# Identity products in an accumulator's unused columns, a new order on VectorE and GpSimd in the first unit, and an early load of a weight block: an attention and mixture-of-experts kernel on one core

## The chip, the cores and the metric

The kernel runs on one core of a Trainium2 chip. The metric is the device time of one execution in microseconds. Three executions took 1271.86, 1272.38 and 1274.48 us; the median is 1272.38 us.

## What is computed

The reference packs keys and values of each head into 32 tokens by an attention with learned queries `p`, lets the real queries attend to these 32, and sends the result through a mixture of four experts whose gates `domain_probs` are given.

```python
def sm_attn(qq, kk, vv):
    s = scale * np.matmul(qq, kk.transpose(0, 1, 3, 2))
    a = np.exp(s - np.max(s, axis=-1, keepdims=True))
    a = a / (np.sum(a, axis=-1, keepdims=True) + 1e-09)
    return np.matmul(a, vv)
p_packed = sm_attn(p, k, v)
x = sm_attn(q, p_packed, p_packed)      # then heads beside each other: (N, D)
...
gate = domain_probs / (domain_probs.sum(-1, keepdims=True) + 1e-09)
for e in range(E):
    h = np.maximum(x @ w1[e], 0.0)
    out += gate[:, e:e + 1] * (h @ w2[e])
```

There are 8 batches, 8 heads, 576 positions and head width 64, so 4608 tokens of width 512; 4 experts of inner width 1024. All is fp32.

## The kernel before

**Products.** Every large matrix product is made of three fp32r products: an operand is split into a high part (a cast) and a low part (operand minus high part). `hi_of` (L149) and `lo_of` (L154) record the two steps, `x` becomes `xh` and `xl`, and so on.

**Units.** The eight blocks of 512 inner columns (`ch`, four experts by two) and the eight batches make units `(pair of batches, ch, batch)`, written out in `units` (L403). The first four are (block 0, batch 0), (block 1, batch 0), (block 1, batch 1), (block 0, batch 1). A unit has a first product and a second.

The first is `x @ w1` for 288 tokens (`c`, a half of a batch) and 256 inner columns (`kh`), a group of 12 matmuls, by `mm1_group` (L422). `w1` is not taken raw: since x is made of the 32 packed tokens, `g_form` (L370) multiplies the packed tokens with `w1` to a gate matrix `ghl`, and the groups multiply `ghl` with the softmax weights `xh` and `xl`. VectorE then multiplies by the gate (`pbt`) and takes the maximum with zero in one instruction. The four results are the blocks a11, a12, a21 and a22 of the hidden matrix.

The second product is by Strassen's scheme in Winograd's form: seven products (`product`, L535, 12 matmuls each) instead of eight, of sums s1 to s4 of the a blocks (formed at the end of `mm1_group` in the branch a21) with sums t1 to t4 of the four blocks of `w2` (`t_form`, L504). `ORDER` (L35) is the order of the seven: a11, s3, s1, s2, a22, s4, a12. `s_operand` (L472) splits a left operand: the cast on ScalarE, the subtraction on GpSimd (`st`). a12's operand, `stl`, is split on VectorE (`split`, L414). `tt` are the right operands, `rw` the raw blocks of `w2`. Each product is added into one of seven sums `acc` by VectorE, or copied by ScalarE the first time.

**Start.** Before unit 0, `pack_unit` (L187) packs the tokens of batch 0 (transposes of the weights `a`, copies `at`, products with the values `vt`), and `tok_halves` (L303) forms batch 0's softmax weights in two halves of 288 tokens: `turned`, `shifted` and `normed` are a transpose, row maximum and subtraction, and the normalisation. Batch 1's packing (`packs[2:]`) and its tokens (`tok_unit`, L267) come between: as long as unit 0 runs, `back` (L724) hands out two of their steps behind each product.

**Who comes first.** The tile framework schedules each engine's instructions by its own estimate, within the dependences; several wrappers add an order where the schedule is to be fixed. `InOrder` (L61) keeps VectorE (`vq`) or GpSimd (`gq`) in the order of recording while its `on` is set. `vec` notes the last instruction that forms a unit's blocks as "sum"; `avec` is for attention and, while `avec.on` is set, stays behind the last "sum" recorded so far; `bact` does so on ScalarE behind the last "high" part of `s_operand`, and `bpool` on GpSimd behind the last "low" part. TensorE's groups are kept in order by `together` (L121) and `on_pe` (L108). There are four accumulators of two PSUM banks each (`dbl`); a group uses columns 0 to 287 of both banks of 512. `FORM` (L739) tells behind which products of a unit a step of `t_form` for a later block is recorded, `GROUPS_LATE` (L738) behind which products of unit 1 the groups of unit 2 stand (the first behind product 3). SP issues the loads and stores in the order of recording where they wait for the same buffers.

Of the kernel before, what the change touches and what calls it, by code (L numbers as in the profile page):

```python
# [8 lines left out]
F32 = mybir.dt.float32  # L9
# [7 lines left out]
P = 128  # L17
# [4 lines left out]
NG = NPAIR // 2  # L22
SB = B // 2
HS = S // 2
# [9 lines left out]

ORDER = ["a11", "s3", "s1", "s2", "a22", "s4", "a12"]  # L35
NPROD = len(ORDER)


@with_exitstack
def attention_moe(ctx: ExitStack, tc: tile.TileContext, q, k, v, p, dp, w1, w2, out):  # L40
# [7 lines left out]
    xpool = pool("xpool", 2)  # L48
# [27 lines left out]
    vq, gq = InOrder(nc.vector), InOrder(nc.gpsimd)  # L76
# [226 lines left out]
    def tok_halves(b, new):  # L303
        xs[b] = tuple(xpool.tile([P, NG, 2, HP], F32R, name=f"{n}{b // 2 % 2}") for n in ("xh", "xl"))
        qts = []
        for g in range(NG):
            qts.append(new[g](b, [P, 2, S], "qt"))
            nc.sync.dma_start(out=qts[g], in_=q[b][:, 2 * g:2 * g + 2, :])
        yield
        pss = [  # L310
            scores([b], g, lambda b, pr, hh: ppbd[b % 4][hh * D:(hh + 1) * D, pr, :], {b: qts[g]})[b]
            for g in range(NG)
        ]
        yield
        n = HS // 32
        a2s = [new[g](b, [P, 2 * n, NPK], "a1") for g in range(NG)]
        ats = [new[g](b, [P, S], "at") for g in range(NG)]
        def block(g, c):
            return a2s[g][:, c * n:(c + 1) * n]

        def turned(g, c):
            vq.transpose(out=block(g, c).rearrange("p a n -> p (a n)"), in_=pss[g][:, c, 0:HS])

        def shifted(g, c):
            a2 = block(g, c)
            m2 = small.tile([P, n, 1], F32, name="m2")
            vq.tensor_reduce(out=m2, in_=a2, axis=AX.X, op=ALU.max)
            vq.tensor_tensor(out=a2, in0=a2, in1=m2.broadcast_to([P, n, NPK]), op=ALU.subtract)
            nc.scalar.activation(out=a2, in_=a2, func=AF.Exp, scale=SCALE)

        def normed(g, c):
            a2, ts = block(g, c), slice(c * HS, (c + 1) * HS)
            s2 = small.tile([P, n, 1], F32, name="s2")
            vq.tensor_reduce(out=s2, in_=a2, axis=AX.X, op=ALU.add)
            vq.tensor_scalar_add(s2, s2, 1e-9)
            vq.reciprocal(out=s2, in_=s2)
            vq.tensor_tensor(out=a2, in0=a2, in1=s2.broadcast_to([P, n, NPK]), op=ALU.mult)
            vq.transpose(out=ats[g][:, ts], in_=a2.rearrange("p a n -> p (a n)"))
            xh, xl = (t[:, g, c, 0:HS] for t in xs[b])
            hi_of(xh, ats[g][:, ts], nc.scalar)  # L340
            lo_of(xl, ats[g][:, ts], xh, gq)

        for g in range(NG):
            turned(g, 0)
            shifted(g, 0)
        yield
        normed(0, 0)
        for g in range(NG):
            turned(g, 1)
        normed(1, 0)  # L350
        yield
        for g in range(NG):
            shifted(g, 1)
        yield
        for g in range(NG):
            normed(g, 1)
        yield

    def w1_load(ch):
# [52 lines left out]
    blocks = {}  # L412
# [6 lines left out]
        lo_of(st[:, 1], psv, st[:, 0], vec)  # L419
        blocks[u, "op", ORDER.index(name) if name in ORDER else name] = st  # L420

    def mm1_group(u, kh, c):  # L422
        sb, ch, b = units[u]
        xh, xl = xs[b]
        ts = slice(c * HS, (c + 1) * HS)
        ps = dbl()
        for fi in range(2):
            f = 2 * kh + fi
            fs = slice(f * P, (f + 1) * P)
            n = 0  # L430
            for g in range(NG):
                ghl = gs[b, ch][g]
                for hl, rx in ((0, xl), (0, xh), (1, xh)):
                    mm(
                        out=ps[:, fi, 0:HS], lhsT=ghl[:, hl, fs], rhs=rx[:, g, c, 0:HS],
                        start=n == 0, stop=n == 3 * NG - 1,
                    )
                    n += 1
        psv = ps[:, :, 0:HS]

        def held(name):
            tag, bufs = ("ablk", 3) if name[0] == "a" else ("sblk", 4)
            blocks[u, name] = hpool.tile([P, 2, HS], F32, name=tag, bufs=bufs)
            return blocks[u, name]

        def add(dst, x, y, op):
            vec.tensor_tensor(out=dst, in0=x, in1=y, op=op)

        name = f"a{c + 1}{kh + 1}"
        vec.scalar_tensor_tensor(  # L450
            out=held(name) if c == kh else psv, in0=psv, scalar=0.0,
            in1=pbt[b][:, ts].rearrange("p (o t) -> p o t", o=1).broadcast_to([P, 2, HS]),
            op0=ALU.max, op1=ALU.mult,
        )
        if u == len(units) - 1:
            if c != kh:
                split(u, name, psv)
        elif name == "a21":
            add(held("s3"), blocks[u, "a11"], psv, ALU.subtract)
            add(psv, psv, blocks[u, "a22"], ALU.add)  # L460
            add(held("s2"), psv, blocks[u, "a11"], ALU.subtract)
            nc.scalar.copy(out=held("s1"), in_=psv)  # L462
            if (u, "a12") in blocks:
                add(held("s4"), blocks[u, "a12"], blocks[u, "s2"], ALU.subtract)
        elif name == "a12":
            if (u, "s2") in blocks:
                add(held("s4"), psv, blocks[u, "s2"], ALU.subtract)
            else:
                blocks[u, "a12"] = psv
            split(u, name, psv)  # L470

    def s_operand(u, i):  # L472

# [30 lines left out]
    def t_form(ch, first=False):  # L504
# [7 lines left out]
        steps = (  # L512
            ("a11", "t1", "t3"), ("s3", "s1", "t2"), ("s2", "t4"), ("a22",), ("s4",), ("a12",),
        )
        how = {"t1": ("b12", "b11", "b11"), "t2": ("b22", "t1", "t1"), "t3": ("b22", "b12", "b12"), "t4": ("t2", "b21", "t2")}
        for names in steps:
            for name in names:
# [135 lines left out]
    def drain(gen):  # L653
        for _ in gen:
            pass
# [6 lines left out]
    with ExitStack() as first:  # L662
# [42 lines left out]
            next(gen)  # L705
        next(halves)
        drain(fold)
        next(halves)
        next(forms)
        mm1_group(0, 0, 0)  # L710
        s_operand(0, 0)
        next(halves)
        mm1_group(0, 1, 0)
        for gen in packs[2:]:
            next(gen)
        mm1_group(0, 1, 1)
        mm1_group(0, 0, 1)
        s_operand(0, 1)
        vq.on = gq.on = False
        drain(forms)  # L720

    apool = ctx.enter_context(tc.tile_pool(name="apool", bufs=2, reuse_waits="tile"))

# [12 lines left out]
    GROUPS = {1: ((0, 0),), 3: ((1, 1),), 4: ((0, 1),), 6: ((1, 0),)}  # L736
    GROUPS_FIRST = {2: ((0, 0),), 3: ((1, 1),), 4: ((0, 1),), 6: ((1, 0),)}
    GROUPS_LATE = {3: ((0, 0),), 4: ((1, 1),), 5: ((0, 1),), 6: ((1, 0),)}  # L738
    FORM = {0: (0, 2, 3, 4, 5, 6), 2: (6,), 3: (0, 1, 2, 3, 4)}  # L739
    for kh in range(2):  # L740
        w2_load(1, kh, raw_tile)
    tsteps = nothing
    kind = None
    sums, late, back = nothing, False, second_batch()
    for u, (sb, ch, b) in enumerate(units):
        pos = u % (2 * NCH)
        odd = pos % 2 == 1
        opening = u < 4
        nxt = units[u + 1] if u + 1 < len(units) else None

        if u == 1:
# [26 lines left out]
        for i in range(NPROD):  # L778
# [23 lines left out]
                next(back, None)  # L802
            elif i == 5 and kind != "scores" or i == 2 and u > 2 or i == 0 and odd and u > 3:
                kind = next(back, None)
            if i in form_at:
                next(tsteps, None)
            if u == 1 and i < 2:
                w2_load(2, i, raw_tile)
# [54 lines left out]
```

## Time and profile before

| | |
|---|---|
| three executions | 1271.86, 1272.38, 1274.48 us |
| the profiled execution: time, span | 1272.35 us, 1270.6 us |
| mean granted TensorE clock | 0.997 |
| TensorE busy | 1247.0 us (98%) |
| VectorE, ScalarE, GpSimd busy | 926.1 us (73%), 496.1 (39%), 735.8 (58%) |
| moved by DMA | 213.98 MB, 168 GB/s on average |

The page and the views that answer to questions name engines PE (TensorE matmul), PEld (its weight load), DVE (VectorE), ACT (ScalarE), POOL (GpSimd) and SP (which issues DMAs). A row of the timeline is start, duration, engine, line, operation, `out<-in`, shape and count, and in brackets the idle time ahead of it with the instruction that ended it. A line can be that of a wrapper (L68, L116), so rows are told apart by their tiles.

### The profile page before, as it was taken

To read this page: it belongs to the slowest core of one execution; us is meant where nothing else is said; L and a number is where in the kernel's file an instruction comes from. 1 tells how busy PE (TensorE), PEld (TensorE's weight loads), DVE (VectorE), ACT (ScalarE), POOL (GpSimd) and SP (SyncE) were. 2 spreads that over 40 slices of the span, in tenths; PEclk is the share of its full clock that TensorE was granted. 3 is DMA by queue.
4 is the path that set the end of the run, shared out by engine and by line. 5 is a ranking of instruction groups with operands and counts; after the bars stand their busy time and mean duration, and the time that the engine had idled before them with its cause. 6 is when DMAs were issued, how large, how long until landed. Compare 5 with 4: busy or idle time off the path is not lost.

```text
span 1270.6 us, 26902 instructions
## 1 busy us (share of the span) xinstructions
PE 1247.0 (98%) x10732; PEld 1166.7 (92%) x10732; DVE 926.1 (73%) x1389; ACT 496.1 (39%) x847; POOL 735.8 (58%) x529
## 2 busy tenths in 40 slices
PE   6899999999999999999999999999999999999998
PEld 3789899999999999999999999999999999999998
DVE  6675676788876667888777676788877567766766
ACT  2554445344435233343335433243343533323331
POOL 3876978798675344455466344364557545445456
PEclk9899999999999999999999999999999999999999
DMA  9665575536466444555345555433445543444322
GB/s 339 242 250 200 218 236 177 193 123 213 161 211 209 163 160 127 181 175 165 125 150 175 175 196 165 159 115 116 159 159 182 159 139 116 123 151 159 126 67 76
DMA packets 86508, 213.98 MB, mean 168 GB/s; under 512 B 8816, under 2 KB 27632, under 8 KB 86384
## 3 DMA queue, kind: packets, MB, share of 16 engines
q1 hardware_dynamic: 85712, 212.11, 50.3%
q8 instruction: 86, 1.41, 0.5%
q14 instruction: 38, 0.31, 0.1%
q10 hardware_dynamic: 672, 0.15, 0.1%
HBM read 173.35 MB, written 38.87 MB: 167 GB/s over the span
## 4 chain that ended last, share of the span: by engine, by line
PE 91%; POOL 2%; DMA 2%; DVE 2%; issue 1%; ACT 0%; SPq 0%; DVEq 0%; POOLq 0%; ACTq 0%
PE dbl L116 85%; PE dbl L124 6%; POOL st L68 1%; DMA rw<-in_w 1%; PE dbl L119 1%; DMA pbt<-pnd 1%; DMA vt<-in_v 1%; DVE a L68 1%; POOL tt L68 1%; POOL acc L68 0%; DVE dbl L68 0%; DVE sblk L68 0%; DVE s L68 0%; POOL rw L68 0%; ACT st L151 0%
## 5 line engine op out<-in xcount | busy, mean ns | idle before, releaser
L116 PE MATMUL dbl<-st,tt 128*128 128x288 f32 x4608 | 665.7, 295 | 3.5 <-DVE acc L68 1.8
L116 PEld LDWEIGHTS dbl<-st,tt 128*128 128x128 f32 x4608 | 623.1, 188 | 38.6 <-POOL st L68 19.2
L68 POOL TENSOR_TENSOR st<-sblk,st 128x576 fp32r<-128x576 f32 x252 | 364.7, 1458 | 435.9 <-ACT st L151 434.6
L116 PE MATMUL dbl<-xh,ghl 128*128 128x288 f32 x2048 | 414.4, 295 | 0.0
L68 DVE TENSOR_TENSOR acc<-dbl,acc 128x576 f32<-128x576 f32 x390 | 292.3, 750 | 93.0 <-PE dbl L116 90.6
L116 PEld LDWEIGHTS dbl<-xh,ghl 128*128 128x128 f32 x2048 | 328.9, 189 | 0.2 <-DVE ghl L68 0.2
L116 PE MATMUL dbl<-xl,ghl 128*128 128x288 f32 x1024 | 303.3, 296 | 6.0 <-POOL xl L68 5.7
L151 ACT CAST st<-sblk 128x576 fp32r<-128x576 f32 x252 | 164.1, 675 | 362.6 <-DVE sblk L68 290.9
L68 POOL TENSOR_TENSOR st<-ablk,st 128x576 fp32r<-128x576 f32 x128 | 187.2, 1463 | 47.8 <-ACT st L151 47.7
L116 PEld LDWEIGHTS dbl<-xl,ghl 128*128 128x128 f32 x1024 | 193.1, 189 | 8.7 <-POOL xl L68 6.4
L68 DVE SCALAR_TENSOR_TENSOR dbl<-dbl,pbt 128x576 f32<-128x576 f32 x128 | 97.8, 764 | 75.7 <-PE dbl L116 74.5
L68 DVE SCALAR_TENSOR_TENSOR ablk<-dbl,pbt 128x576 f32<-128x576 f32 x128 | 96.4, 753 | 65.5 <-PE dbl L116 63.0
L151 ACT CAST st<-ablk 128x576 fp32r<-128x576 f32 x128 | 86.1, 674 | 123.7 <-PE dbl L116 92.4
L116 PE MATMUL dbl<-stl,tt 128*128 128x288 f32 x780 | 114.6, 296 | 0.0
L116 PEld LDWEIGHTS dbl<-stl,tt 128*128 128x128 f32 x780 | 105.9, 188 | 0.2
L68 DVE TENSOR_TENSOR ghl<-dbl,ghl 128x512 fp32r<-128x512 f32 x128 | 84.9, 685 | 25.9 <-ACT ghl L151 25.9
L151 ACT CAST ghl<-dbl 128x512 fp32r<-128x512 f32 x128 | 72.2, 590 | 52.9 <-DVE ghl L68 52.2
L68 POOL TENSOR_TENSOR tt<-rw,tt 128x512 fp32r<-128x512 f32 x57 | 74.2, 1321 | 18.7 <-ACT tt L85 18.7
L68 DVE TENSOR_TENSOR stl<-dbl,stl 128x576 fp32r<-128x576 f32 x64 | 48.4, 756 | 39.5 <-ACT stl L151 39.5
L124 PE MATMUL dbl<-wraw,ppbd 64*32 64x512 f32 x1024 | 67.7, 595 | 0.9 <-DMA wraw<-in_w 0.9
L462 ACT COPY sblk<-dbl 128x576 f32<-128x576 f32 x63 | 40.4, 642 | 64.1 <-DVE sblk L68 64.1
L552 ACT COPY acc<-dbl 128x576 f32<-128x576 f32 x56 | 35.9, 641 | 50.9 <-PE dbl L116 50.8
(64 smaller groups left out, 703.1 us busy)
## 6 DMA issues: line engine op xcount, KB each, us to landing
tt<-td SPq DMA_DIRECT2D x175, 512.0 KB, 4.3
wraw<-in_w SPq DMA_DIRECT2D x132, 256.0 KB, 4.3
td<-tt SPq DMA_DIRECT2D x56, 512.0 KB, 5.0
pbt<-pnd SPq DMA_DIRECT2D x32, 288.0 KB, 3.9
out<-acc SPq DMA_DIRECT2D x31, 288.0 KB, 2.6
rw<-in_w SPq DMA_DIRECT2D x16, 512.0 KB, 5.8
kt<-in_k SPq DMA_DIRECT2D x14, 576.0 KB, 5.2
kt<-in_q SPq DMA_DIRECT2D x14, 576.0 KB, 5.8
```

Of the source, the lines that this page charges most:

```text
L68: res = getattr(self.eng, op)(*args, **kw)
L116: on_pe(nc.tensor.matmul(**kw))
L119: on_pe(nc.tensor.transpose(**kw))
L124: ins = nc.tensor.matmul(**kw).ins
L151: return eng.copy(out=dst, in_=src)
L462: nc.scalar.copy(out=held("s1"), in_=psv)
L552: nc.scalar.copy(out=accs[b, i], in_=psv)
```

## The change

- **Identity products.** `mm1_group` takes a number `idle`. For the group of a12 in unit 0 it is `IDLE = 23`: so many fp32 products of the identity with itself, 128 columns wide, go to columns 288 to 415 of the second bank of a12's accumulator, which nothing reads. They are recorded with `together` behind that group, so the two groups of the second token half stay behind them, and a12's multiply on VectorE, which works on the same tile, waits for the last of them.
- **Order of VectorE and GpSimd in the first unit.** a11's operand and a12's split are recorded later, `normed` of the second half is cut in two steps, `t_form`'s second step is cut in two for block 0, and operands 1 to 3 of unit 0 are recorded before the rest of block 0's `t_form`. `avec.on` is set before unit 0 and stays set, `bact.on` is set for the rest of block 0's `t_form` only, and `gq.on` stays set through unit 0. Block 1's `t_form` steps stand behind products 3, 3, 4, 5, 6 and 6 of unit 0 instead of 0, 2, 3, 4, 5 and 6.
- **Block 1's W2.** Its two raw halves go to the two buffers named `xh1`, which hold batch 1's keys, instead of the buffers `rw0` and `rw1` that hold block 0's.

```diff
+IDLE = 23
@@ tok_halves
-        yield
-        for g in range(NG):
-            normed(g, 1)
+        normed(0, 1)
+        yield
+        normed(1, 1)
@@ mm1_group(u, kh, c, idle=0)
+        if idle:
+            together([
+                dict(out=ps[:, 1, HS:HS + P], lhsT=ident, rhs=ident, start=True, stop=True) for _ in range(idle)
+            ])
...
                 add(held("s4"), psv, blocks[u, "s2"], ALU.subtract)
+                split(u, name, psv)
             else:
                 blocks[u, "a12"] = psv
-            split(u, name, psv)
@@ t_form
+        if first:
+            steps = steps[:1] + (("s3", "s1"), ("t2",)) + steps[2:]
@@ before unit 0
         drain(fold)
+        next(forms)
         next(halves)
         next(forms)
         mm1_group(0, 0, 0)
+        next(halves)
         s_operand(0, 0)
-        next(halves)
-        mm1_group(0, 1, 0)
+        mm1_group(0, 1, 0, IDLE)
+        next(forms)
         for gen in packs[2:]:
             next(gen)
+        split(0, "a12", blocks[0, "a12"])
         mm1_group(0, 1, 1)
         mm1_group(0, 0, 1)
-        s_operand(0, 1)
-        vq.on = gq.on = False
+        for i in range(1, 4):
+            s_operand(0, i)
+        avec.on = bact.on = True
+        vq.on = False
         drain(forms)
+        bact.on = False
...
-    FORM = {0: (0, 2, 3, 4, 5, 6), 2: (6,), 3: (0, 1, 2, 3, 4)}
+    FORM = {0: (3, 3, 4, 5, 6, 6), 2: (6,), 3: (0, 1, 2, 3, 4)}
     for kh in range(2):
-        w2_load(1, kh, raw_tile)
+        w2_load(1, kh, lambda shape, name: xpool.tile(shape, F32, name="xh1"))
@@ each unit
+        gq.on = u == 0
...
-            if i in form_at:
+            for _ in range(form_at.count(i)):
                 next(tsteps, None)
```

The order of the built instructions shows where they come to stand. The first place is VectorE while unit 0 ends and unit 1's a21 is formed; `a_781` and `a_793` are batch 1's two token tiles, `m` their row maxima, `s` their row sums. Before:

```order
L68 STREAM_TRANSPOSE a_781<-dbl 128x288 x2
L68 TENSOR_REDUCE m_837<-a_781 128x18
L68 STREAM_TRANSPOSE a_793<-dbl 128x288 x2
L68 TENSOR_TENSOR a_781<-a_781,m_837 128x576
L68 TENSOR_REDUCE m_841<-a_793 128x18
L68 TENSOR_TENSOR a_793<-a_793,m_841 128x576
L68 SCALAR_TENSOR_TENSOR dbl<-dbl,pbt 128x2x288
L68 TENSOR_REDUCE s_867<-a_781 128x18
L68 TENSOR_TENSOR sblk<-ablk,dbl 128x576
L68 TENSOR_TENSOR dbl<-dbl,ablk 128x2x288
```

After, at the same place (the tiles are `a_792` and `a_804`):

```order
L69 STREAM_TRANSPOSE a_792<-dbl 128x288 x2
L69 STREAM_TRANSPOSE a_804<-dbl 128x288 x2
L69 SCALAR_TENSOR_TENSOR dbl<-dbl,pbt 128x2x288
L69 TENSOR_TENSOR sblk<-ablk,dbl 128x576
L69 TENSOR_TENSOR dbl<-dbl,ablk 128x2x288
L69 TENSOR_TENSOR sblk<-dbl,ablk 128x576
L69 TENSOR_REDUCE m_856<-a_792 128x18
L69 TENSOR_REDUCE m_860<-a_804 128x18
L69 TENSOR_TENSOR a_792<-a_792,m_856 128x576
L69 SCALAR_TENSOR_TENSOR dbl<-dbl,pbt 128x2x288
L69 TENSOR_TENSOR a_804<-a_804,m_860 128x576
```

The maxima and subtractions moved from ahead of a21's multiply (the first `SCALAR_TENSOR_TENSOR`) to behind it and the three sums that follow from it.

The second place is VectorE a little later, where the finished tokens are transposed into `at` and unit 1's products are added into `acc`. Before, from the addition of product 0 on:

```order
L68 TENSOR_TENSOR acc_574<-dbl,acc_574 128x576
L68 STREAM_TRANSPOSE at<-a_781 128x576
L68 TENSOR_TENSOR ghl<-dbl,ghl 128x512
L68 TENSOR_TENSOR stl<-dbl,stl 128x2x288
L68 TENSOR_TENSOR ghl<-dbl,ghl 128x512
L68 TENSOR_TENSOR acc_638<-dbl,acc_638 128x576
L68 TENSOR_TENSOR acc_703<-dbl,acc_703 128x576
L68 TENSOR_TENSOR acc_752<-dbl,acc_752 128x576
L68 STREAM_TRANSPOSE at<-a_793 128x576
```

After, from the same `ghl` on; between the addition of product 0 (`acc_603`) and these rows stand the row sums `s` of both tiles and `stl`:

```order
L69 TENSOR_TENSOR ghl<-dbl,ghl 128x512
L69 RECIPROCAL s_892<-s_892 128x18
L69 TENSOR_TENSOR ghl<-dbl,ghl 128x512
L69 TENSOR_TENSOR acc_659<-dbl,acc_659 128x576
L69 TENSOR_TENSOR a_792<-a_792,s_887 128x576
L69 TENSOR_TENSOR a_804<-a_804,s_892 128x576
L69 TENSOR_TENSOR acc_721<-dbl,acc_721 128x576
L69 STREAM_TRANSPOSE at<-a_792 128x576
L69 TENSOR_TENSOR acc_763<-dbl,acc_763 128x576
L69 STREAM_TRANSPOSE at<-a_804 128x576
```

The first `at` moved from behind the addition of product 0 to behind that of product 2, the second stays behind that of product 3.

The third place is ScalarE in batch 1's packing, the two pairs of copies `at` (whole tile and rest) that TensorE's second pass reads. Before:

```order
L85 COPY at<-dbl 128x512
L85 COPY at<-dbl 64x128
L552 COPY acc_638<-dbl 128x576
L151 CAST st<-sblk 128x2x288
L85 COPY at<-dbl 128x512
```

After:

```order
L86 COPY at<-dbl 128x512
L86 COPY at<-dbl 64x128
L86 CAST tt<-rw_183 128x512 x2
L86 CAST tt<-xh_586 128x512
L559 COPY acc_659<-dbl 128x576
L152 CAST st<-sblk 128x2x288
L86 COPY at<-dbl 128x512
```

Three casts of W2 blocks moved in between the pairs; before, two of them stood ahead of unit 0's first product and one behind the second pair. On GpSimd the subtractions that give the second half's two `xl` moved ahead of a11's `st`, each directly behind a W2 step, and the operands s3, s1 and s2 of unit 0 moved ahead of the last cast and the last three subtractions of block 0's W2.

More of the change, by code (lines that the diff above doesn't have):

```diff
@@ L420, in split, with mm1_group @@
         blocks[u, "op", ORDER.index(name) if name in ORDER else name] = st
-    def mm1_group(u, kh, c):
+    def mm1_group(u, kh, c, idle=0):
         sb, ch, b = units[u]
```

## The prediction

> **What bounds the kernel now.** I read the page first: its span and its busy shares.
>
> ```profile
> span 1270.6 us, 26902 instructions
> PE 1247.0 (98%) x10732; PEld 1166.7 (92%) x10732; DVE 926.1 (73%) x1389; ACT 496.1 (39%) x847; POOL 735.8 (58%) x529
> ```
>
> The profiled execution took 1272.35 us, 1.75 more than its span; the median of the runs shown is 1272.38, so sums made against the profile need no correction. TensorE is busy 98% of the span and sets the time: what it waits, or runs at a slower clock, is lost. So I next asked for the windows view, cut where the start-up ends, and then for the timeline of TensorE there.
>
> ```profile
> 28.50:40.63 12.13, 6.34 (x26) 5.66 (x25) 9.57 (x22) 4.86 (x10) 10.83 (x11) 0.72 0.96 359
> 58.30:85.30 27.00, 25.21 (x204) 22.89 (x193) 22.44 (x35) 12.54 (x21) 20.45 (x15) 1.00 0.85 309
> ...
> 28.09 0.43 PE L116 MATMUL dbl<-xh,ghl 128*128 128x288 f32 x2
> 34.19 0.61 PE L116 MATMUL dbl<-xl,ghl 128*128 128x288 f32 x1 [5.67 <-POOL xl L68]
> 40.63 1.74 PE L116 MATMUL dbl<-st,tt 128*128 128x288 f32 x12
> 49.38 0.65 PE L116 MATMUL dbl<-xl,at 128*32 128x64 f32 x32 [0.96 <-ACT at L85]
> 72.62 4.98 PE L116 MATMUL dbl<-st,tt 128*128 128x288 f32 x36 [1.79 <-DVE acc L68]
> 77.44 0.29 PE L116 MATMUL dbl<-xl,ghl 128*128 128x288 f32 x1
> 81.78 0.29 PE L116 MATMUL dbl<-xl,ghl 128*128 128x288 f32 x1
> ```
>
> The columns of the windows are the length, the busy time of PE, weight load, VectorE, ScalarE and GpSimd, then the granted clock, the DMA share and GB/s. A large loss lies in 28.5 to 40.6: it waits 5.67 us for the second half of batch 0's tokens (`xl`), and then works at a low clock. Later waits are 0.96 at 49.38 and 1.79 at 72.62. At 77.44 and 81.78 it takes up the two halves of batch 1's `xl` without a wait. The 36 products from 72.62 to 77.44 give 0.134 us for one 288-column product at full clock.
>
> **The idle block.** No plain fp32 product of 128 columns stands in the trace. An fp32 product is two records there, so 23 are 46 records. The grouped rows give the length of one record at 512 and at 288 columns.
>
> ```profile
> L124 PE MATMUL dbl<-wraw,ppbd 64*32 64x512 f32 x128 | 13.1, 595 | 0.9 <-DMA wraw<-in_w 0.9
> L124 PE MATMUL dbl<-kt,ppbd 64*32 64x288 f32 x32 | 2.1, 405 | 0.0
> ...
> 44.70 1.31 PE L119 MATMUL dbl<-ident,a 128*128 128x128 f32 x10 [0.48 <-ACT sblk L462]
> ```
>
> 190 ns for 224 columns more is 0.85 ns a column, 0.109 us for 128, 5.0 us for 46. Ten transposes of that width in 1.31 us give 6.0 as the other end. I take 5.2: the block lasts from 28.5 to 33.7, inside the old wait. It adds one wait: a12's multiply on VectorE now waits for its last product. Behind that multiply stand the row maxima of batch 1's first scores, whose exponentials on ScalarE free the accumulator that a21 needs.
>
> **The second half's tokens.** These VectorE and GpSimd rows set the old wait.
>
> ```profile
> 26.87 0.46 DVE L68 TENSOR_TENSOR a<-a,m 128x288 f32<-128x288 f32 x1
> 28.17 0.76 DVE L68 SCALAR_TENSOR_TENSOR ablk<-dbl,pbt 128x576 f32<-128x576 f32 x1 [0.84 <-DMA pbt<-pnd]
> 28.85 0.44 DVE L68 TENSOR_REDUCE s<-a 128x9 f32<-128x288 f32 x1
> 30.02 1.34 DVE L68 TENSOR_TENSOR a<-a,s 128x288 f32<-128x288 f32 x1
> 31.80 0.41 DVE L68 TENSOR_REDUCE s<-a 128x9 f32<-128x288 f32 x1
> 33.52 0.48 DVE L68 STREAM_TRANSPOSE at<-a 128x288 f32<-128x288 f32 x1
> ...
> 36.04 0.74 DVE L68 TENSOR_REDUCE nb<-dbl 128x1 f32<-128x576 f32 x1
> ...
> 37.01 0.74 ACT L85 ACTIVATE a<-dbl,nb 128x576 f32<-128x576 f32 x1 [1.68 <-DVE nb L68]
> ```
>
> Normalising one head group took 2.95 us with a slow `a<-a,s` (28.85 to 31.80) and 2.2 without (31.80 to 34.00). Now it starts at 27.35, with a11's multiply (0.68 to the next start) between the two groups: the second transpose ends between 27.35 + 2 x 2.2 + 0.68 = 32.4 and 33.9. The block's 33.7 and this chain end within 0.3 us of each other, so a12's multiply starts at about 33.9. From there 0.68 to the maxima, 0.97 from them to the exponential, and 0.78 for it: a21's products start at 36.35, and 12 at full clock end at 38.0. Product 0 started at 40.63, so **2.6 us** are won here (2.1 to 2.9 for a block of 6.0 to 5.0 us). GpSimd, which now takes `xl` first, and block a22 are ready before that.
>
> **The casts on ScalarE.** In the second pass of batch 1's packing TensorE waits for the `at` copies. Three casts of W2 blocks now stand between the first pair and the second.
>
> ```profile
> 38.59 1.13 ACT L85 CAST tt<-rw 128x512 fp32r<-128x512 f32 x2
> 46.72 0.75 ACT L85 COPY at<-dbl 128x512 f32<-128x512 f32 x2
> 47.63 0.64 ACT L552 COPY acc<-dbl 128x576 f32<-128x576 f32 x1 [0.16 <-PE dbl L116]
> ```
>
> The first pair ends at 47.47 - 2.6 = 44.87. The casts add 1.7 (1.13 for two), and copy, cast and copy the old 1.75 (47.63 to 49.38): TensorE goes on at 48.3, not 49.38. Of the gain **1.0 us** is left; if the casts cost nothing it would be 2.6.
>
> **VectorE in unit 1.** From 49.38 to 62.66 the old TensorE rows have no wait, so that stretch moves by 1.0. Here the new order on VectorE decides.
>
> ```profile
> 62.23 0.43 PE L116 MATMUL dbl<-xh,ghl 128*128 128x288 f32 x2
> ...
> 58.39 0.85 DVE L68 STREAM_TRANSPOSE a<-dbl 128x288 f32<-128x288 f32 x2 [0.31 <-PE dbl L124]
> 60.70 0.72 DVE L68 TENSOR_TENSOR a<-a,m 128x576 f32<-128x576 f32 x1
> 70.52 1.29 DVE L68 TENSOR_TENSOR a<-a,s 128x576 f32<-128x576 f32 x1
> 72.40 0.76 DVE L68 STREAM_TRANSPOSE at<-a 128x576 f32<-128x576 f32 x1
> 73.09 0.65 DVE L68 TENSOR_TENSOR ghl<-dbl,ghl 128x512 fp32r<-128x512 f32 x1
> 74.93 0.73 DVE L68 TENSOR_TENSOR acc<-dbl,acc 128x576 f32<-128x576 f32 x1
> ...
> 73.19 0.67 ACT L85 CAST xh<-at 128x576 fp32r<-128x576 f32 x1 [1.44 <-DVE at L68]
> 75.83 1.43 POOL L68 TENSOR_TENSOR xl<-at,xh 128x576 fp32r<-128x576 f32 x1
> ```
>
> Before, VectorE ran batch 1's row maxima and shifts while TensorE was still forming a21 (its last product ends at 62.66). Now they stand behind a21's multiply, which needs that product: VectorE idles for 2.6 us after the four transposes and starts again at 62.7 - 1.0 = 61.7. Ahead of the first `at` it has the old work of 58.39 to 73.16, 14.8 us, without the two pairs of transposes (1.7), with `ghl`, `stl`, `ghl` and an `acc` (73.09 to 75.66, 2.5) and one more `acc` (0.7): 16.3 us. `at` ends at 78.0, not 73.16. The cast (0.7) and GpSimd's subtraction (1.47) put the first `xl` at **80.2**; TensorE took it at 77.44. The second `at` reuses the buffer of the first, so it waits for that subtraction: 0.8 + 0.7 + 1.5 more give **83.25**, against 81.78. At that point the new order has 13 products fewer behind it (10 of product 5 and 3 of a21 come after), 1.7 us. So the kernel stands 83.25 + 1.7 - 81.78 = **3.2 us later** than before.
>
> In between the first `acc` leaves VectorE at 69.8 (11 instructions, nine of 0.68 and two of 0.72 and 1.26), so the wait at 72.62 does go: products 1 to 3 start 2.7 us earlier, end at about 75.3 after 0.7 us for `stl`, and TensorE then stands still for 4.9 us. What is late next is batch 1's `xl`.
>
> The largest uncertainty is four subtractions and multiplications that read two SBUF operands, rows of 0.72 to 1.29 us. All at 0.72 take 1.3 off the 4.2 that I carry, all at 1.29 add 1.0. [...]
>
> **GpSimd.** It now forms the low parts of s3, s1 and s2 ahead of the last three W2 operands, so the operands of a22 and s4 come behind a cast and three subtractions more.
>
> ```profile
> 48.54 1.41 POOL L68 TENSOR_TENSOR st<-ablk,st 128x576 fp32r<-128x576 f32 x1
> 59.22 1.86 PE L116 MATMUL dbl<-st,tt 128*128 128x288 f32 x12
> ```
>
> a22's was ready at 49.95 and is used at 59.22. Four instructions of at most 1.41 are 5.6 us, inside the 9.3 less the 1.0 that TensorE is early: no cost.
>
> **W2 in the key buffers.** Two 512 KB loads now follow the four `wraw` loads.
>
> ```profile
> 28.45 3.83 SPq L364 DMA_DIRECT2D wraw<-in_w  x4
> wraw<-in_w SPq DMA_DIRECT2D x4, 256.0 KB, 6.2
> ```
>
> They used to stand behind four stores that wait for GpSimd. The last `wraw` lands by about 32.3 + 6.2 = 38.5, and TensorE needs it at 38.0 + 12 x 0.134 = 39.6: no cost. What hides them is 1.1 us of slack. At 359 GB/s 1 MB is 2.9 us; if the loads share the engines with `wraw`, up to 1.8 us of that delays batch 0's second gate matrix. The stores that now come behind them are read again only in unit 2.
>
> **Sum.** 1272.35 + 3.2 = **1275.5 us**; behind that point the engines' orders are alike and each instruction starts on another engine's event, none at a fixed time, so the delay is kept. Bounds of this case: -1.3 and +1.0 from VectorE, +1.8 from the loads, -1.6 if the casts are free; singly, 1273.9 to 1277.3.
>
> **Rivals.**
> *The clock halves in the new gap.* These windows show the old one.
>
> ```profile
> 32.00:34.00 2.00, 0.00 (x0) 0.00 (x0) 1.86 (x6) 0.34 (x1) 2.00 (x3) 0.85 1.05 395
> 40.00:41.00 1.00, 1.00 (x8) 1.00 (x8) 0.17 (x1) 0.00 (x0) 1.00 (x2) 0.89 0.18 74
> ```
>
> The last product ended at 28.52. With half the clock, the means of 0.85 and 0.89 put the drop at 33.4, 4.9 us later, and the return at 40.2 (6.8 us at half, as the mean of 0.72 over 28.5 to 40.63 has it too). My gap is 4.9 us long, on the edge. A drop just ahead of its end, as the old one was, would cost 6.0 us at half speed, 3.0 lost, less 0.6 that the wait for the second `xl` absorbs: 1277.9. [...]
>
> *VectorE packs better, or the casts are free* (both low ends): 3.2 - 1.3 - 1.6 = 0.3, with some of each 1273.2. The span is then within what can be told from no change. For it: VectorE is busy 22.44 of 27 us, not full.
>
> *Batch 1's tokens are not waited for, and the kernel is faster.* It decides at 75.3: if the first `at` ends by 73.1, TensorE never stops, and it keeps the 2.7 us of the first `acc`, and up to 4.4 with free casts: about 1269. For it speaks that before, `at` ended at 73.16. Against it, the written order would need 16.3 us of rows in 11.4.
>
> *The change does not do what it says:* the identity products do not hold the clock, or take twice the time. Twice is 5.2 us more before a12's multiply, 1279 to 1281; without the clock a21 takes 1.3 us longer, 1276.8.
>
> **How the numbers follow.** Forecast 0.40, clock 0.25, packs better 0.22, faster 0.08, does not do it 0.05. A measurement of this kernel can tell about 0.2%, 2.5 us, from no change: below 1269.8 is faster, above 1274.9 slower. Two thirds of the forecast case, the clock case and the last case are above: 0.27 + 0.25 + 0.05 = 0.57. Faster: 0.08, and 0.02 from the casts. Same: 0.33. The range of 1272.5 to 1279.0 leaves out the faster case, the lower edge of the better packing and the doubled block, under 0.2.
>
> **What would show it.** Right: the 5.67 us wait gone, clock 1.00 in 34 to 40, product 0 near 38.0; a wait of 2 to 3 us for `at` at 48; none at 70; then 4 to 5 us for `xl` near 75 to 80. Wrong: no such wait there, `at` before 75 us, or product 0 after 40.

## The result and the profile after

The changed kernel takes 1278.59 us in the median of eight executions (1276.70 to 1281.65), the kernel before 1272.68 in eight beside them (1271.86 to 1274.48). The ratio is 1.0051, with a 95% interval of 1.0042 to 1.0060: it is slower, by about 6 us. The forecast had 3.2.

The profiled execution is the fastest of the eight, 1276.70 us: 4.35 more than the profiled one before. Its page begins:

```profile
span 1274.9 us, 26998 instructions
...
PE 1250.8 (98%) x10778; PEld 1171.3 (92%) x10778; DVE 927.7 (73%) x1389; ACT 495.9 (39%) x847; POOL 734.6 (58%) x529
```

The places of which the prediction spoke, from the timeline of TensorE after the change:

```profile
28.06 5.30 PE L125 MATMUL dbl<-ident 128*128 128x128 f32 x46
...
35.01 0.40 PE L117 MATMUL dbl<-xl,ghl 128*128 128x288 f32 x1 [1.26 <-POOL xl L69]
...
37.88 1.74 PE L117 MATMUL dbl<-st,tt 128*128 128x288 f32 x12
...
47.91 0.65 PE L117 MATMUL dbl<-xl,at 128*32 128x64 f32 x32 [2.25 <-ACT at L86]
...
66.43 1.85 PE L117 MATMUL dbl<-st,tt 128*128 128x288 f32 x12 [0.49 <-POOL st L69]
...
72.30 3.39 PE L117 MATMUL dbl<-st,tt 128*128 128x288 f32 x24 [0.25 <-DVE stl L69]
80.45 0.40 PE L117 MATMUL dbl<-xl,ghl 128*128 128x288 f32 x1 [4.76 <-POOL xl L69]
...
80.97 3.08 PE L117 MATMUL dbl<-st,tt 128*128 128x288 f32 x12
...
84.74 0.29 PE L117 MATMUL dbl<-xl,ghl 128*128 128x288 f32 x1
...
94.83 1.92 PE L125 MATMUL dbl<-wraw,ppbd 64*32 64x512 f32 x16
```

The old wait of 5.67 us is filled but for 1.26 us, product 0 starts at 37.88 instead of 40.63, the wait for `at` has become 2.25 us long, the wait for `acc` (1.79 us at 72.62 before) is gone, and a new wait of 4.76 us for batch 1's `xl` stands ahead of 80.45. At 84.74 TensorE takes the second `xl`. The last row, the gate matrix that is formed in unit 2, serves as a mark. Before the change it stood here:

```profile
90.17 1.92 PE L124 MATMUL dbl<-wraw,ppbd 64*32 64x512 f32 x16
```

It is 4.66 us later, and from it to the end of the span are 1180.4 us before and 1180.1 after. All of the difference is made ahead of the mark, and so it is in every experiment below (1179.9 to 1180.5 us behind it).

VectorE, GpSimd and ScalarE show why the two waits are there. VectorE, from batch 1's transposes to its second `at`, and GpSimd's second `xl`:

```profile
56.92 1.82 DVE L69 STREAM_TRANSPOSE a<-dbl 128x288 f32<-128x288 f32 x4 [0.31 <-PE dbl L125]
61.29 0.77 DVE L69 SCALAR_TENSOR_TENSOR dbl<-dbl,pbt 128x576 f32<-128x576 f32 x1 [2.55 <-ACT acc L559]
...
77.46 0.76 DVE L69 STREAM_TRANSPOSE at<-a 128x576 f32<-128x576 f32 x1
...
80.44 0.78 DVE L69 STREAM_TRANSPOSE at<-a 128x576 f32<-128x576 f32 x1 [1.57 <-POOL xl L69]
...
82.00 1.41 POOL L69 TENSOR_TENSOR xl<-at,xh 128x576 fp32r<-128x576 f32 x1 [1.60 <-ACT xh L86]
```

ScalarE, with the three casts between the two pairs of copies:

```profile
43.97 0.75 ACT L86 COPY at<-dbl 128x512 f32<-128x512 f32 x2
44.60 1.15 ACT L86 CAST tt<-rw 128x512 fp32r<-128x512 f32 x2
45.64 0.63 ACT L86 CAST tt<-xh 128x512 fp32r<-128x512 f32 x1
...
47.27 0.76 ACT L86 COPY at<-dbl 128x512 f32<-128x512 f32 x2
```

VectorE idles 2.55 us ahead of a21's multiply and ends its first `at` at 78.22. The row names a copy of ScalarE, but that had ended at 60.29; a21's last product on TensorE ends at 61.20, just ahead of the multiply. The windows view shows the clock (after PE, weight load, VectorE, ScalarE and GpSimd comes the granted clock). The first row is the stretch with the identity products; the others are three stretches of 3.41 us around the new wait, cut where the clock changes.

```profile
28.50:38.00 9.50, 8.24 (x69) 8.01 (x68) 8.56 (x15) 3.84 (x8) 6.68 (x7) 1.00 1.06 385
74.10:77.52 3.42, 1.59 (x13) 1.36 (x11) 3.42 (x6) 0.00 (x0) 1.48 (x2) 1.00 0.75 288
77.52:80.93 3.41, 0.47 (x3) 0.48 (x4) 1.84 (x4) 0.67 (x1) 1.40 (x1) 1.00 0.01 4
80.93:84.35 3.42, 3.42 (x17) 3.42 (x16) 0.55 (x2) 0.67 (x1) 2.35 (x2) 0.50 0.00 0
```

The identity products hold the clock at 1.00. Behind the new wait it is 0.50 for 3.42 us, and the twelve products at 80.97 take 3.08 us there instead of 1.74. The stretch ahead of the half clock was not empty: TensorE worked 0.47 us in it.

This profile is the mildest of the eight executions. Each comes with its mean clock:

| time, us | 1276.70 | 1277.49 | 1277.97 | 1278.33 | 1278.86 | 1278.96 | 1281.34 | 1281.65 |
|---|---|---|---|---|---|---|---|---|
| mean clock | 0.999 | 0.997 | 0.996 | 0.996 | 0.995 | 0.995 | 0.993 | 0.993 |

A mean lower by 0.006 is about 15.3 us more at half clock (2 x 0.006 x 1275), and goes with 4.95 us more time, about a third. The means have three digits, and count half clock at the very end of a span as well (before the change the last 1.55 us, from 1269.05 on, have a clock of 0.50), so such figures are estimates. The profile has 3.41 us at half clock where the mean of the eight, 0.9955, stands for 11.5, so it shows less of the loss than the median execution has.

### The profile page after: what moved, and what is told of

Its sections match the earlier page's. It is cut to its first block, busy times and chain, and to the rows that moved or that the text cites. A ratio compares the mean times of both kernels' runs of the same rounds, so it can differ in the third digit from the quotient of the medians.

```text
span 1274.9 us, 26998 instructions
## 1 busy us (share of the span) xinstructions
PE 1250.8 (98%) x10778; PEld 1171.3 (92%) x10778; DVE 927.7 (73%) x1389; ACT 495.9 (39%) x847; POOL 734.6 (58%) x529
## 3 DMA queue, kind: packets, MB, share of 16 engines
q8 instruction: 86, 1.41, 0.4%
## 4 chain that ended last, share of the span: by engine, by line
PE 92%; DVE 3%; POOL 2%; issue 1%; ACT 1%; DMA 1%; DVEq 0%; SPq 0%; POOLq 0%; ACTq 0%
PE dbl L117 85%; PE dbl L125 6%; POOL st L69 1%; PE dbl L120 1%; DVE a L69 1%; DVE s L69 1%; POOL tt L69 0%; POOL acc L69 0%; DMA kt<-in_k 0%; ACT st L152 0%; DMA td<-tt 0%; DVE sblk L69 0%; DVE m L69 0%; DVE dbl L69 0%; POOL xl L69 0%
## 5 line engine op out<-in xcount | busy, mean ns | idle before, releaser
L69 POOL TENSOR_TENSOR tt<-rw,tt 128x512 fp32r<-128x512 f32 x50 | 65.2, 1320 | 16.0 <-ACT tt L86 15.9
```

The lines of the kernel that those rows point to most:

```text
L69: res = getattr(self.eng, op)(*args, **kw)
```

## Experiments

Theory A: the loss has two sources, the tokens of batch 1 that stand behind on VectorE and the casts on ScalarE ahead of the second `at` pair; both make TensorE wait, and the clock halves behind such a wait. Rivals: the identity products, the load or GpSimd's order are the cost. Ratios are against the kernel before in the same runs; the change itself has 1.0051.

| kernel | median, us | ratio, 95% interval |
|---|---|---|
| after, tokens free (e1_avec) | 1275.95 | 1.0029 (1.0018 to 1.0041) |
| after, only the shift free (e15_shift) | 1275.07 | 1.0024 (1.0015 to 1.0034) |
| after, casts later (e9_casts) | 1274.74 | 1.0014 (1.0005 to 1.0023) |
| after, both (e9_best) | 1272.40 | 0.9997 (0.9989 to 1.0006) |
| both, GpSimd free (e13_gq_best) | 1275.86 | 1.0022 (1.0013 to 1.0030) |
| after, 18 products in the new wait (e2_fill18) | 1277.23 | 1.0032 (1.0020 to 1.0045) |
| after, 9 products there (e2b_fill9) | 1277.02 | 1.0036 (1.0024 to 1.0048) |
| after, no identity products (e3_idle0) | 1280.47 | 1.0058 (1.0045 to 1.0072) |
| after, old buffers for W2 (e6_w2) | 1280.02 | 1.0052 (1.0039 to 1.0065) |
| before, identity products (e4_before_idle) | 1277.88 | 1.0042 (1.0029 to 1.0055) |
| before, products, load, casts later (e10_idle_key_casts) | 1271.86 | 0.9992 (0.9984 to 1.0001) |
| the same again (e10_again) | 1272.17 | 0.9998 (0.9987 to 1.0008) |

### Tokens free on VectorE

```diff
-        avec.on = bact.on = True
+        bact.on = True
         vq.on = False
         drain(forms)
```

> The kernel after, but avec.on stays off in unit 0 as before the change, so that batch 1's row maxima, shifts and normalisation may run on VectorE ahead of a21's sums. Theory A (the tokens behind on VectorE make the 4.8 us wait for xl at 75.7 to 80.5, and the clock halves behind that wait): the first transpose into at ends by 73, there is no wait for xl over 1 us, no half clock behind it, and the kernel keeps between 1.0 us (the casts take the rest) and 2.8 us of what the start gained: 1269.5 to 1271.7, mean clock 0.998 or more in every run. Rival B (the loss is in the identity products, the W2 load or GpSimd's order): within 1 us of the kernel after, 1276 to 1280.

1275.95 us: better than after, and worse than expected. TensorE and the windows view of this kernel:

```profile
48.73 0.85 PE L117 MATMUL dbl<-xl,at 128*32 128x64 f32 x32 [2.25 <-ACT at L86]
...
75.13 6.52 PE L117 MATMUL dbl<-st,tt 128*128 128x288 f32 x36 [2.97 <-DVE acc L69]
```

```profile
45.63:49.04 3.41, 1.16 (x63) 0.91 (x65) 0.28 (x1) 3.21 (x7) 3.33 (x4) 1.00 0.00 0
49.04:52.45 3.41, 3.41 (x42) 2.82 (x32) 0.28 (x1) 0.00 (x0) 3.41 (x4) 0.50 0.91 247
```

The first `at` ends at 71.9 and the wait for `xl` is gone as expected, but in its place TensorE waits 2.97 us for the first `acc`, since a21's sums now share VectorE with the tokens; half clock follows that wait too (0.50 from 76.34 to 79.76). And here the wait of 2.25 us for `at` was enough to halve the clock: the stretch ahead of the half clock had 1.16 us of work in 3.41.

The same with the maxima and subtractions alone let go:

```diff
+            ahead = vq if b == 1 else avec
-            avec.tensor_reduce(out=m2, in_=a2, axis=AX.X, op=ALU.max)
-            eng.tensor_tensor(out=a2, in0=a2, in1=m2.broadcast_to([P, S // 32, NPK]), op=ALU.subtract)
+            ahead.tensor_reduce(out=m2, in_=a2, axis=AX.X, op=ALU.max)
+            ahead.tensor_tensor(out=a2, in0=a2, in1=m2.broadcast_to([P, S // 32, NPK]), op=ALU.subtract)
```

> The kernel after, with nothing but batch 1's row maxima and subtractions let go ahead of a21's multiply on VectorE (the normalisation stays behind it); TensorE's order is that of after. Theory A as the forecast had it (VectorE's 2.5 us of idle time ahead of a21's multiply is what the new order wastes): the first at ends 2.5 us earlier, at 75.7, the wait for xl falls from 4.8 to 2 us or less. As the additions into acc then come behind the normalisation, TensorE waits for the first acc instead, by 2 to 3 us near 71: 1275.5 to 1277. Rival (the wait for xl alone sets the loss, and acc is not waited for): 1275.0 or less.

1275.07 us. TensorE, and VectorE's first `at`:

```profile
74.42 6.47 PE L117 MATMUL dbl<-st,tt 128*128 128x288 f32 x36 [2.63 <-DVE acc L69]
```

```profile
74.86 0.76 DVE L69 STREAM_TRANSPOSE at<-a 128x576 f32<-128x576 f32 x1
```

The first `at` ends 2.6 us earlier than after (75.62 against 78.22), which is the idle time ahead of a21's multiply; `acc` is waited for instead, as expected. The median is 0.4 below the range that theory A gave and just above the rival's; the wait for `acc` that the rival denied is there.

### Casts behind the second pair of copies

The last two steps of block 0's `t_form`, s4 and a12, are recorded behind product 0 of unit 0. `bact` gets a second key, the last copy of the second `at` pair, and is on for W2's casts in that unit.

```diff
-    bact, bpool = Behind(nc.scalar, "high"), Behind(gq, "low")
+    bact, bpool = Behind(nc.scalar, "high", "copies"), Behind(gq, "low")
...
+        next(forms)
+        next(forms)
         avec.on = bact.on = True
         vq.on = False
-        drain(forms)
         bact.on = False
...
+            bact.on = bact.on or u == 0
+            if u == 0 and i == 0:
+                drain(forms)
             for _ in range(form_at.count(i)):
                 next(tsteps, None)
+            bact.on = bact.on and u > 0
```

> The kernel after, with two of the three casts of W2 blocks on ScalarE put behind the second pair of at copies in unit 0. Theory A: TensorE's wait for at goes on 1.15 us earlier (46.8 instead of 47.9), and as a21's product and with it VectorE's chain start earlier, xl comes 1.15 us earlier too: 1.15 less than after, median 1277.4, still with the wait of 4.5 to 5 us for xl. Rival E (VectorE's chain is set by something that does not start with a21's product): xl at 80.4 as before, no gain.

1274.74 us, 3.85 less than after where 1.15 was expected. TensorE:

```profile
47.00 0.65 PE L117 MATMUL dbl<-xl,at 128*32 128x64 f32 x32 [1.21 <-ACT at L86]
...
67.08 2.02 PE L117 MATMUL dbl<-st,tt 128*128 128x288 f32 x12 [2.08 <-POOL st L69]
...
78.52 0.40 PE L117 MATMUL dbl<-xl,ghl 128*128 128x288 f32 x1 [0.56 <-POOL xl L69]
...
91.75 1.92 PE L125 MATMUL dbl<-wraw,ppbd 64*32 64x512 f32 x16
```

The wait for `at` is 1.04 us shorter, as worked out. The first `xl` comes 1.93 earlier rather than 1.15, since VectorE now transposes `at` ahead of an addition. The rest is put down to the clock, as an estimate: the mean over the executions is 0.9979, against 0.9955 of after, which is 6 us less at half clock (2 x 0.0024 x 1275), and by the third that such time cost above, 2 us. A wait of 2.08 us for `st` is new here, and half clock (0.50) follows it in this profile (68.58 to 71.99).

Both edits together, the lines ahead of unit 0 then being:

```diff
+        next(forms)
+        next(forms)
-        avec.on = bact.on = True
         vq.on = False
-        drain(forms)
-        bact.on = False
```

> The kernel after with both edits undone in part: avec.on off in unit 0 and two of three W2 casts behind the second pair of at copies. Theory A: no at wait over 1.3 us, so that no window near 46 is half idle, and tokens not late; the 1275.95 of the first edit alone falls by 1.1 us of casts and by about 1 us of half clock: 1273.8 (1272.5 to 1274.8), mean clock 0.997 or more. Rival F (the two edits gain the same thing): no better than 1274.7, what the casts alone gave.

1272.40 us, within 0.1% of before. What the two gain by themselves, 0.0022 and 0.0037 of the ratio, adds up to 0.0059; together they gain 0.0054. So with both places undone the net loss is gone, while the start keeps what it gained. What is left is a wait for GpSimd in unit 1:

```profile
67.78 2.72 PE L117 MATMUL dbl<-st,tt 128*128 128x288 f32 x12 [2.46 <-POOL st L69]
```

I took that for GpSimd's fixed order and gave it up, with the old `FORM` of unit 0:

```diff
-        gq.on = u == 0
-    FORM = {0: (3, 3, 4, 5, 6, 6), ...
+    FORM = {0: (0, 2, 3, 4, 5, 6), ...
-        vq.on = False
+        vq.on = gq.on = False
```

> The kernel after with three edits: avec.on off in unit 0, two of three W2 casts behind the second pair of at copies, and gq.on off in unit 0 with the old places of block 1's W2 steps, so that GpSimd may take a unit's operands ahead of block 1's W2. Theory A: the wait of 2.5 us for st at 65, which is left in the kernel with the first two edits (1272.40), goes, and with it a window under half busy in 0.6 of the executions: 1.5 to 3 us less, 1270.0 (1269 to 1271.5), faster than before. Rival (GpSimd's order costs nothing, as I predicted): 1272.4 as with two edits.

That failed: 1275.86 us. GpSimd and TensorE:

```profile
73.55 3.75 POOL L69 TENSOR_TENSOR tt<-xh,tt 128x512 fp32r<-128x512 f32 x3
77.26 1.40 POOL L69 TENSOR_TENSOR xl<-at,xh 128x576 fp32r<-128x576 f32 x1
```

```profile
78.71 0.61 PE L117 MATMUL dbl<-xl,ghl 128*128 128x288 f32 x1 [3.38 <-POOL xl L69]
```

Three subtractions for block 1's W2 now stand directly ahead of the first `xl`, and TensorE waits 3.38 us for it. So GpSimd's order and `FORM` in the change, with what the estimate does elsewhere when they are given up, are worth 3.5 us by the medians (0.0025 of the ratio, 3.2 us) where the tokens are early.

### Work in the new wait

18 identity products go ahead of unit 2's first group, in its accumulator's unused columns. Product 4 thereby comes ahead of that group on TensorE.

```diff
+        if ahead:
+            together([
+                dict(out=ps[:, 1, HS:HS + P], lhsT=ident, rhs=ident, start=True, stop=True) for _ in range(ahead)
+            ])
         for fi in range(2):
...
-                    mm1_group(u + 1, *grp)
+                    mm1_group(u + 1, *grp, ahead=FILL if (u, i) == (1, 3) else 0)
```

> The kernel after, with 18 more identity products ahead of unit 2's first group, in unused columns of its accumulator: 4.2 us of work for TensorE in the 4.8 us in which it waits for xl. VectorE's order is as after, so the wait's end stays. Theory A with the clock (what the median loses beyond the forecast is half clock behind that wait): the clock stays at 1.00 there, 1.7 us of the profiled execution's loss goes (3.41 us at half), 1275.0 in nearly every run, spread under 1 us. Rival C (the excess over the forecast is a longer stall, not the clock): the same as after, median 1278 and a spread of 4 us. Rival D (the clock drops elsewhere, at the start): spread and mean clock as after.

1277.23 us; two of the five executions had a mean clock of 0.999 and took 1275.62 and 1275.82, three had 0.997 and took 1277.23 to 1277.48. The spread fell from 4.95 to 1.86, which speaks against rivals C and D, though it is five executions against eight and the two intervals overlap. The profiled one is of the slower three:

```profile
77.39 4.18 PE L126 MATMUL dbl<-ident 128*128 128x128 f32 x36
81.32 1.83 PE L118 MATMUL dbl<-st,tt 128*128 128x288 f32 x12
```

```profile
45.81:49.22 3.41, 1.16 (x64) 0.91 (x68) 0.28 (x1) 3.16 (x7) 3.33 (x4) 1.00 0.00 0
49.22:52.63 3.41, 3.41 (x41) 2.82 (x30) 0.28 (x1) 0.00 (x0) 3.41 (x4) 0.50 0.91 234
```

Behind the new wait the clock stays at 1.00. What is left in this profile is half clock behind the `at` wait, and a stretch of it from 11.67 to 15.09, behind a window with 1.51 us of work (two short waits for ScalarE's `a`, 0.58 and 1.32 us). My expectation of 1275.0 left both out. Nine products instead of 18:

```diff
-FILL = 18
+FILL = 9
```

> The kernel after with 9 identity products ahead of unit 2's first group instead of 18: 2.1 us of work in the wait for xl of 4.8 us, which leaves at most 2.7 us without work in one piece, less than a window of 3.41 us. If the clock halves only behind a window without any work, it never halves behind this wait: time as with 18, 1277.2 or less. If it halves behind a window with under about 1.5 us of work (what the windows of the runs so far have), it still does in some 0.6 of the executions: between 18 products and none, 1277.3 to 1278.6, with executions at a mean clock of 0.996 or less among them.

1277.02 us, from 1275.11 to 1279.54. Neither theory is favoured: the median fits the first, an execution at a mean clock of 0.996 the second, and the profiled one has half clock from 12.0 to 18.8 and none behind the new wait, where its emptiest window has 1.74 us of work.

### The identity products left out, and alone

```diff
-IDLE = 23
+IDLE = 0
```

> The kernel after without the identity products. Theory A (they hold the clock through the wait for the second half's xl and cost nothing): two windows at half clock between 31 and 40, product 0 about 2 us later than 37.9, 1280 (1279 to 1282). Rival B (they are a cost, since a12's multiply and what is behind it on VectorE wait for the last of them): product 0 at 38 or earlier, 1276 to 1277.5.

1280.47 us, as theory A had it, though its interval overlaps with that of after. TensorE:

```profile
33.74 0.61 PE L117 MATMUL dbl<-xl,ghl 128*128 128x288 f32 x1 [3.41 <-DVE s L69]
...
37.14 0.61 PE L117 MATMUL dbl<-xl,ghl 128*128 128x288 f32 x1 [2.31 <-POOL xl L69]
...
42.35 2.00 PE L117 MATMUL dbl<-st,tt 128*128 128x288 f32 x12
```

Product 0 is 4.5 us later than after, 2.1 of them because this execution, the slowest of its six, reached its first group at 26.79 instead of 24.67. The clock is 0.50 from 32.66 to 42.90 here and was 1.00 there after the change: the products do hold it, and no cost of them is seen.

The kernel before with the products alone:

```diff
+IDLE = 23
...
+        if idle:
+            together([
+                dict(out=ps[:, 1, HS:HS + P], lhsT=ident, rhs=ident, start=True, stop=True) for _ in range(idle)
+            ])
         psv = ps[:, :, 0:HS]
...
-        mm1_group(0, 1, 0)
+        mm1_group(0, 1, 0, IDLE)
```

> The kernel before, with the 23 identity products behind a12's group and nothing else. Theory A (the products hold the clock and cost nothing): clock 1.00 from 28 to 40; a22 from 34.2 at full clock ends 1.7 us later, a21 starts when its accumulator is free at 37.8 and ends at 39.4, product 0 at 39.4 instead of 40.63: 1.2 us faster, 1271.1. Rival B (the products are the cost, since VectorE waits for the last of them): product 0 not before 40.6, 1273 to 1278.

1277.88 us: the expectation was wrong by 6.8. Product 0 starts at 40.43, 14.64 us behind the first group (25.79), where before it was 15.65 behind (24.98 to 40.63): the gain of 1.0 is there. But the 23 products change the estimate by which the framework schedules the other engines, and ScalarE's order with it:

```profile
46.53 0.75 ACT L86 COPY at<-dbl 128x512 f32<-128x512 f32 x2
49.90 0.62 ACT L86 CAST tt<-rw 128x512 fp32r<-128x512 f32 x1 [2.62 <-DMA rw<-in_w]
...
51.52 0.74 ACT L86 COPY at<-dbl 128x512 f32<-128x512 f32 x2
```

A cast of block 1's W2 now stands ahead of the second pair and waits 2.62 us for its load, and TensorE waits 3.94 us for `at`:

```profile
52.17 0.65 PE L117 MATMUL dbl<-xl,at 128*32 128x64 f32 x32 [3.94 <-ACT at L86]
```

That is neither A nor B, but a third thing: an order that goes wrong elsewhere. With the load early and the casts behind the copies (`bact` with its second key, as above) it is put right:

```diff
-        w2_load(1, kh, raw_tile)
+        w2_load(1, kh, lambda shape, name: xpool.tile(shape, F32, name="xh1"))
             if i in form_at:
+                bact.on = bact.on or u == 0
                 next(tsteps, None)
+                bact.on = bact.on and u > 0
```

> The kernel before with three things added: the 23 identity products behind a12's group, block 1's W2 loaded early into the key buffers, and the casts of block 1's W2 put behind batch 1's second pair of at copies. The order of VectorE and GpSimd is that of before. Theory A (what the start gains is 1 us or more, and the loss comes from VectorE's order and from waits behind which the clock halves): product 0 at 39.6 or earlier on a start like that of before, no wait for at over 1.2 us, no new wait for xl, 1271.2 (1270 to 1272.3), so faster than before by up to 0.1% or 0.2%. Rival B (the identity products or the load cost more than they bring): 1273 or more.

```profile
40.32 1.74 PE L117 MATMUL dbl<-st,tt 128*128 128x288 f32 x12
...
49.08 0.65 PE L117 MATMUL dbl<-xl,at 128*32 128x64 f32 x32 [0.96 <-ACT at L86]
...
72.31 4.97 PE L117 MATMUL dbl<-st,tt 128*128 128x288 f32 x36 [1.80 <-DVE acc L69]
...
89.86 1.92 PE L125 MATMUL dbl<-wraw,ppbd 64*32 64x512 f32 x16
```

1271.86 us at 0.9992. The same kernel was timed again:

> The same kernel as the one before with identity products, early load and casts behind the copies, timed again beside the kernel before, since its ratio of 0.9992 had an interval that reached 1.0001. If it is faster: 1271.9 and a ratio of 0.999, with an interval that ends below 1. If not: a ratio within 0.0005 of 1.

1272.17 us at 0.9998: no difference from before that can be told. The wait for `acc` is as long as before, 1.80 us. From the first group to the mark both profiles of this kernel take 1.0 us less than before (64.16 and 64.17 against 65.19), but their first groups come 0.72 and 0.56 us later (25.70 and 25.54 against 24.98). No version tried beats the kernel before.

### The load

```diff
-        w2_load(1, kh, lambda shape, name: xpool.tile(shape, F32, name="xh1"))
+        w2_load(1, kh, raw_tile)
```

> The kernel after, with block 1's W2 loaded into its old buffers again, behind the stores. The estimate then puts one cast of block 1 behind the second pair of at copies instead of ahead of it. My prediction put the load at no cost: within 1 us of after, 1277.6 to 1279.6, of which the one cast gives back 0.6. Rival G (the early load carries the first unit, since GpSimd's work on block 1 is what unit 1's first products wait for): slower than after by over 1.5 us, 1280 or more, with waits for st near 66. Rival H (the early load delays the gate matrix or the tokens): faster, 1276.5 or less.

1280.02 us, a ratio of 1.0052 against 1.0051. TensorE:

```profile
47.57 0.65 PE L117 MATMUL dbl<-xl,at 128*32 128x64 f32 x32 [1.73 <-ACT at L86]
...
69.16 3.25 PE L117 MATMUL dbl<-st,tt 128*128 128x288 f32 x12 [3.57 <-POOL st L69]
```

One cast fewer stands ahead of the second pair, and unit 1's product 0 waits 3.57 us for GpSimd, which got block 1's W2 later. The profile is what rival G says; the time can't tell it from no cost.

## Why the prediction was right in its steps and wrong in its size

- **The idle block:** right. It took 5.30 us (5.2 forecast) and held the clock (1.00 from 28.50 to 38.00); product 0 started 2.75 us earlier (2.6). The rival that it does not hold the clock, or takes twice the time, is refuted.
- **The casts on ScalarE:** right at full clock. TensorE went on at 47.91 (48.3), so 1.47 us were left of the gain (1.0). The price was too small: 1.6 us for all three, where taking two away gave 3.85, 1.04 of it in that wait.
- **VectorE in unit 1:** right. a21's multiply at 61.29 (61.7), idle 2.55 (2.6), first `at` 78.22 (78.0), first `xl` waited for until 80.45 (80.2), wait 4.76 (4.9), no wait for `acc`. The four instructions that were the largest uncertainty took 1.30, 1.18 and 2.03 for two, 4.5 us in all (4.2 carried).
- **The step from there to 3.2 us later:** too small by 1.46, since the mark is 4.66 later. In the profiled execution this is the half clock behind the wait. The second `xl` was ready at 83.41 (83.25 forecast), but the twelve products ahead took 3.08 us instead of 1.74, so TensorE came to it only at 84.74. From there to the mark it does the 76 products that the forecast counted.
- **The step that failed** is the half clock, for which the sum of 1275.5 us has no term: full clock was the likeliest case (0.40), and half clock a rival of 0.25, by my estimate, at one place, for 1277.9. All eight executions have a mean clock below 1, and the mean of the eight stands for 11.5 us at half clock; by the third above that is some 3.8 us, where the sum had nothing. As an estimate, a straight line through the eight comes to about 1275 us at a clock of 1.00, so the rest of the sum was near right. The kernel before has about as much half clock (a mean of 0.9961 in 17 executions): by these means the change took away that at 33 to 40 and brought about as much back elsewhere, and the sum counted only the first. So the rival was the likelier case. That its price was good to 0.7 us is luck: the profile, with half clock at the place it names, has 3.41 us of it, not 6.0, and took 1276.70; the two executions at the median have mean clocks of 0.996 and 0.995, so 10 to 13 us.
- **The condition for half clock** is what misled me: the drop that I went by came 4.9 us after the last product (28.52 to 33.4 before the change), so I asked for that long a stretch without any work, and put my gap of 4.9 us "on the edge". The runs show half clock behind less: windows of 3.41 us with 1.16 us of work (tokens free, ahead of 49.04) and 1.50 (casts later, ahead of 68.58) were followed by it. So the wait for `at`, which I priced as plain time, is a second such place: half clock followed it in four of the six profiles in which it is 2.25 us long.
- **GpSimd's order and the W2 load at no cost:** right in so far as neither was shown to cost anything. GpSimd's order, with its `FORM`, was worth some 3 us where it was given up.
- **The rival that the change makes the kernel faster** was refuted: it needed the first `at` by 73.1, and that ended at 78.22.

As an estimate of how often: windows of 3.41 us were laid over each profiled execution at 69 starting points, and those with under 1.54 us of work counted between 7 and 140 us (18 of the 19 such windows in the section on the hardware were followed by half clock). There are 1.6 in the kernel before, all at its old wait, 1.9 after the change (0.6 at the `at` wait, 1.3 at the new one), 0.5 with the casts later, and none with the products, load and late casts on the kernel before, though one profile of that kernel has half clock from 11.73 to 15.14, behind a window with 1.58 us. How the median's loss divides between the two places wasn't measured by itself.

## What to carry to other kernels

A wait on TensorE cost more than its length here when the clock halved behind it (behind 4.76 us, twelve products took 3.08 us instead of 1.74), and waits of 2.08 and 2.25 us were enough for that in some executions: price every new wait over some 2 us with a stretch at half clock, and read several executions' clocks rather than one profile's. Before a step is put "behind what is needed first", look at what the engine would do in its idle time there: 2.6 us of VectorE's were given away ahead of a21's multiply. And instructions that only fill time can change the order of the other engines where an estimate sets it.

## What the runs showed of the hardware

In 13 profiles (all but that of e10_again) every window of 3.41 us, laid end to end, has a granted clock of 0.50 or 1.00, with one, two or three windows at 0.50 in a row, and the place of these against the program differs from run to run. From 7 us on and without each profile's last, all 13 full-clock windows with under 1.3 us of TensorE work (0.00 to 1.29 us) were followed by 0.50, none of the 30 with 2.0 to 2.3 us, and 9 of the 26 between (1.41 to 1.98 us of work in those nine). Windows at 0.50 that were busy for 1.09 to 2.50 us were followed by another; busier ones, of 3.01 to 3.42 us, by 1.00, but for two ahead of 16 us (3.35 and 3.36 us). The six profiles in which the clock halves at 11.49 to 12.18 us, around waits for ScalarE's `a` of at most 1.3 us, reach the first group of hidden products at 25.47 to 27.07 us, the seven others at 24.67 to 25.39. A kernel that isn't changed spreads as well: before ranged from 1270.78 to 1276.30 in the 23 executions beside e10_again. Whether it is this half clock that makes it spread is not shown, as its one profile has none there (1.00 from 2.68 to 33.40).
